# Fused attention and two feed-forward blocks on one core: sums of the exponentials with a DVE addition, and other queues

## The chip, the cores and the metric

One core of one Trainium2 chip. The metric is the device time of the kernel in microseconds (us), median over runs. Engines: PE (TensorE matmul; PEld is its weight load), DVE (VectorE), ACT (ScalarE), POOL (GpSimd) and SP (SyncE, which here only issues DMAs).

## The reference

Attention with a tanh cap over 2 x 12 heads (sequence 448, head size 64), then two feed-forward blocks without biases (768 to 2048 to 768), the first with h·cos(h), the second with silu. All in float32, to float32 accuracy.

```python
scores = scale * np.matmul(q, k.transpose(0, 1, 3, 2))
scores = cap * np.tanh(scores / cap)
scores = scores - np.max(scores, axis=-1, keepdims=True)
attn = np.exp(scores)
attn = attn / (np.sum(attn, axis=-1, keepdims=True) + 1e-09)
o = np.matmul(attn, v)                 # then heads side by side: x, (896, 768)
h = x @ w_in;   x2 = (h * np.cos(h)) @ w_out
h = x2 @ w2_in; y  = (h / (1.0 + np.exp(-h))) @ w2_out
```

## The kernel before, in words

The 24 heads go in 12 pairs p; the two heads u of a pair share the 128 partitions. The order of every engine's work is written out by hand (a manual schedule), so each engine's queue is the order of the code.

**Scores.** Keys of a head are cut into three blocks of 128 and a rest of 64. `S_pe(p, t)` computes scores transposed (keys on partitions, the 448 queries on the free axis). For t = 0 to 2 these are block t of both heads, one PSUM bank per head, from q and k split in two float32r parts (`qk_split`, L215 and L216 on DVE): three products per head, each on 64 rows of the array, the two heads on the two row halves (L232). For t = 3 it is the rest of both heads in one bank, straight from `raw` in float32, on two column halves (L236). `ps_s` has three buffers of two banks; a fourth score tile waits for the tanh of the first. `S_tanh` (L244) and `S_exp` (L250) on ACT leave the exponentials in `e32[p]`, seven chunks of 448: chunk 2t+u is block t of head u, chunk 6 the rest, head 0 on partitions 0 to 63 and head 1 on 64 to 127. No maximum is subtracted, since the cap bounds the scores.

**P·V and sums.** `PV(p, steps)` (L262) adds V-transposed times the exponentials into the bank `po`: per step t two float32 matmuls, head u on column half u. Step 3 uses chunk 6 for both heads, with V chunks 6 and 7, whose other half is zeros. `PV_sums` (L275) makes the sums over the keys with matmuls of ones into the bank `sm`: two steps of four matmuls, each on a quarter of 32 columns; quarter c belongs to head c // 2, and the two quarters of a head are added later on DVE. `ps_o` has one bank for `po` and one for `sm`. A float32 matmul leaves two records in the trace, so a step of P·V has four and a step of sums eight.

**Evacuation and normalising.** `evac` copies `po` (L281), `evac_sums` copies `sm` (L286) and sends one row of each quarter with a DMA of its own from SP's queue (L290), four a pair, to `sums[p]` as 32 partitions of 28. `recip(p)` (L296, L297) adds the two halves, takes the reciprocal, writes it to DRAM (`rs`, L299) and reads it back spread over the partitions (`rb`, two DMAs, L302), all on SP. `norm_mul` and `norm_split` (L308, L315, L316) multiply and split the result into the two float32r parts of `x`, the input of the first matrix product.

**Order of a turn.** A loop over p (L359) is software-pipelined: turn p issues the load of pair p+3 (POOL's queue from pair 3 on), the load of V for p+1 (SP), scores, tanh and exponentials of p+1, `recip(p-2)`, `qk_split(p+2)`, the steps of early weights, normalising of p-3, then P·V, `evac`, sums and `evac_sums` of p. In turn 11 the sums and their evacuation come ahead of P·V, and `recip(10)` ahead of the normalising of pair 8. `early` spreads the preparation of the first three weights (a guard and a hi part on ACT; floor, three bit steps and a lo part on DVE) over turns 2 to 10, and a load of the next weight from POOL.

**Ahead of the loop** pair 0 is made: exponentials in two pieces (chunks 0 to 3, then 4 to 6), a `warm_up` of four matmuls with zeros, P·V steps 0 and 1 and one step of sums.

**Behind the loop** `gemm_in` starts: 36 matmuls (L419) with `x` of batch 0 (pairs 0 to 5), 24 with pairs 6 to 9, then 12 with pairs 10 and 11, and so on; from there on the weights stream in and PE works without a break.

Of the kernel before, what the change touches and what calls it, by code (L numbers as in the profile page):

```python
# [28 lines left out]
F32 = mybir.dt.float32  # L29
# [4 lines left out]
ALU = mybir.AluOpType  # L34
# [3 lines left out]
def tile_attention_ffn_ffn(  # L38
# [10 lines left out]
    nc = tc.nc  # L49
    B, H, S, D = shape  # L50
    DM = out.shape[1]
    DFF = w_in1.shape[0] * 128
    P = 128
# [10 lines left out]
    const = ctx.enter_context(tc.tile_pool(name="const", bufs=1))  # L64
# [94 lines left out]
    with ExitStack() as actx:  # L159
        dpool = actx.enter_context(tc.tile_pool(name="dr", bufs=2, space=bass.MemoryType.DRAM))  # L160
        ap_ = actx.enter_context(tc.tile_pool(name="att", bufs=2))
        ps_s = actx.enter_context(tc.tile_pool(name="ps_s", bufs=3, space=PSUM))
        ps_o = actx.enter_context(tc.tile_pool(name="ps_o", bufs=1, space=PSUM))
        NPT = NHEAD // 2
        NCH = 7
        NV = NCH + 1
        Q = 32
        KB = S + 64
        QK = S + KB
        W = 64  # L170
        FULL = S + S // P * P
        FIRST = S + P
        PAD = 16

        raw, vf = {}, {}


        ones = const.tile([P, 3, Q], F32, name="ones")

        def v_init():  # L180
            nc.gpsimd.memset(ones[:, 0], 1.0)
            for u in range(2):
                for h in range(2):
                    nc.gpsimd.memset(ones[h * D:(h + 1) * D, 1 + u], float(u == h))

# [12 lines left out]
        def load_v(p):  # L200
            if p >= NPT:
                return
            vf[p] = ap_.tile([P, NV, D], F32, tag="vf", name=f"vf{p}", bufs=2)
            nc.sync.dma_start(vf[p].rearrange("p c d -> p (c d)"), qkv[p][:, PAD + QK:])

        qh, ql = {}, {}

        def qk_split(p, part=slice(0, FULL)):
            if p >= NPT:
                return  # L210
            if p not in qh:
                qh[p] = ap_.tile([P, FULL], F32R, tag="qh", name=f"qh{p}", bufs=2)
                ql[p] = ap_.tile([P, FULL], F32R, tag="ql", name=f"ql{p}", bufs=2)
            h, x = qh[p][:, part], raw[p][:, PAD:][:, part]
            nc.vector.tensor_copy(h, x)  # L215
            nc.vector.tensor_tensor(out=ql[p][:, part], in0=x, in1=h.bitcast(F32), op=ALU.subtract)  # L216

        sc, e32 = {}, {}

        def S_pe(p, t):  # L220
            if p >= NPT:
                return
            ps = ps_s.tile([P, 2, 512], F32, tag="sc", name=f"sc{p}_{t}")
            sc[p, t] = ps
            h, l = qh.get(p), ql.get(p)
            ops = ((h, h), (h, l), (l, h))
            if t < 3:
                cols = slice(S + t * P, S + (t + 1) * P)
                for m, (kk, qq) in enumerate(ops):
                    for u in range(2):  # L230
                        rows = slice(u * D, (u + 1) * D)
                        nc.tensor.matmul(ps[:, u, :S], kk[rows, cols], qq[rows, :S], start=m == 0, stop=m == 2)  # L232
            else:
                x = raw[p][:, PAD:]
                for c in range(0, P, W):
                    nc.tensor.matmul(ps[c:c + W, 0, :S], x[:, FULL + c:FULL + c + W], x[:, :S], start=True, stop=True)  # L236

        def S_tanh(p, t):
            if p >= NPT:
                return  # L240
            if t == 0:
                e32[p] = ap_.tile([P, NCH, S], F32, tag="e32", name=f"e32_{p}", bufs=2)
            n = 2 if t < 3 else 1
            nc.scalar.activation(out=e32[p][:, 2 * t:2 * t + n, :], in_=sc.pop((p, t))[:, :n, :S], func=AF.Tanh, scale=scap)  # L244

        def S_exp(p, chunks=slice(0, NCH)):
            if p >= NPT:
                return
            e = e32[p][:, chunks, :]
            nc.scalar.activation(out=e, in_=e, func=AF.Exp, scale=capt)  # L250

        po_, sm_ = {}, {}


        def PV(p, steps):
            first = p not in po_
            if first:
                po_[p] = ps_o.tile([P, 512], F32, tag="po", name=f"po{p}")[:, :S]
            for n, t in enumerate(steps):
                for c in range(0, P, W):  # L260
                    u, f = divmod(c, D)
                    nc.tensor.matmul(po_[p][c:c + W], vf[p][:, 2 * t + u, f:f + W], e32[p][:, min(2 * t + u, NCH - 1), :],  # L262
                                     start=first and n == 0, stop=t == 3)


        def PV_sums(p, steps):
            first = p not in sm_
            if first:
                sm_[p] = ps_o.tile([P, 512], F32, tag="sm", name=f"sm{p}")[:, :S]
            for n, t in enumerate(steps):  # L270
                for c in range(4):
                    u, x = divmod(c, 2)
                    chunk = 4 * t + 2 * x + u
                    one = ones[:, 0] if chunk < NCH - 1 else ones[:, 1 + u]
                    nc.tensor.matmul(sm_[p][c * Q:(c + 1) * Q], one, e32[p][:, min(chunk, NCH - 1), :], start=first and n == 0, stop=t == 1)  # L275

        xu, sums, rb = {}, {}, {}

        def evac(p):
            xu[p] = ap2.tile([P, S], F32, tag="xu", name=f"xu{p}", bufs=4)  # L280
            nc.vector.tensor_copy(xu[p], po_.pop(p))  # L281

        def evac_sums(p):
            x = ap2.tile([P, S], F32, tag="xs", name=f"xs{p}", bufs=2)
            sums[p] = ap2.tile([32, 2, S // 16], F32, tag="sums", name=f"sums{p}", bufs=2)
            nc.vector.tensor_copy(x[:3 * Q + 1], sm_.pop(p)[:3 * Q + 1])  # L286
            for u in range(2):
                for y in range(2):
                    at = u * D + y * Q
                    nc.sync.dma_start(sums[p][16 * u:16 * u + 16, y], x[at:at + 1])  # L290

        def recip(p):
            if p < 0:
                return
            s = sums.pop(p)
            nc.vector.tensor_tensor(out=s[:, 0], in0=s[:, 0], in1=s[:, 1], op=ALU.add)  # L296
            nc.vector.reciprocal(out=s[:, 0], in_=s[:, 0])  # L297
            d = dpool.tile([2, S], F32, tag="rs", name=f"rs{p}")
            nc.sync.dma_start(d.rearrange("h (a n) -> (h a) n", a=16), s[:, 0])  # L299
            r = ap2.tile([P, S], F32, tag="rb", name=f"rb{p}", bufs=4)  # L300
            for u in range(2):
                nc.sync.dma_start(r[u * D:(u + 1) * D, :], d[u:u + 1].to_broadcast([D, S]))  # L302
            rb[p] = r

        def norm_mul(p):
            if p < 0:
                return
            nc.vector.tensor_tensor(out=rb[p], in0=xu.pop(p), in1=rb[p], op=ALU.mult)  # L308
# [12 lines left out]
        def warm_up(n, ps):  # L321
            for _ in range(n):
                nc.tensor.matmul(ps, zero[:, :P], zero, start=True, stop=True)


        early = {}
        for w, turn in ((0, 2), (1, 4), (2, 6)):
            for at, *step in ((0, w_guard, w, None), (1, w_floor, w, nc.vector), (1, w_bits, w, 0), (2, w_bits, w, 1), (2, w_bits, w, 2),
                              (2, w_load, w + 2, nc.gpsimd), (3, w_hi, w), (4, w_lo, w)):
                early.setdefault(turn + at, []).append(step)  # L330
        early.setdefault(NPT - 2, []).append((w_guard, 3, None))
        early.setdefault(NPT - 1, []).append((w_floor, 3, nc.gpsimd))
# [16 lines left out]
        for t in range(4):  # L349
            S_pe(0, t)  # L350
            S_tanh(0, t)
            if t == 1:
                S_exp(0, slice(0, 4))
        S_exp(0, slice(4, NCH))
        qk_split(1)
        warm_up(4, ps_o.tile([P, 512], F32, tag="sm", name="warm1")[:, :S])
        PV(0, [0, 1])
        PV_sums(0, [0])
        for p in range(NPT):  # L359
            load(p + 3)  # L360
            if p > 0:
                load_v(p + 1)
            for t in range(3):
                S_pe(p + 1, t)
                S_tanh(p + 1, t)
            S_pe(p + 1, 3)
            S_tanh(p + 1, 3)
            S_exp(p + 1)
            recip(p - 2)
            qk_split(p + 2)  # L370
            for f, *a in early.get(p, []):
                f(*a)
            if p == NPT - 1:
                recip(p - 1)
            norm_mul(p - 3)
            norm_split(p - 3)
            if p == NPT - 1:
                PV_sums(p, [0, 1])
                evac_sums(p)
            PV(p, range(4) if p else [2, 3])  # L380
            evac(p)
            if p < NPT - 1:
                PV_sums(p, [0, 1] if p else [1])
                evac_sums(p)
        norm_mul(NPT - 3)
        norm_split(NPT - 3)
        recip(NPT - 1)
# [263 lines left out]
```

## Time and profile before

| what | us |
|---|---|
| median of 3 runs | 581.74 |
| runs, lowest to highest | 581.37 to 588.43 |
| profiled execution, time | 580.33 |
| profiled execution, span first to last instruction | 578.5 |
| PE busy in the span | 567.1 |
| DVE / ACT / POOL busy | 379.9 / 265.1 / 155.7 |

All rows come from the one profiled execution; its own time (580.33) is its span and what lies around it. In rows, "x16" is a count of records, a mean or the length of a merged group stands in front, and brackets say how long the engine was idle before and what it waited for. Ends of matmuls are modelled; starts are records.

### The profile page before, as it was taken

To read this page: it belongs to the slowest core of one execution; us is meant where nothing else is said; L and a number is where in the kernel's file an instruction comes from. 1 tells how busy PE (TensorE), PEld (TensorE's weight loads), DVE (VectorE), ACT (ScalarE), POOL (GpSimd) and SP (SyncE) were. 2 spreads that over 40 slices of the span, in tenths; PEclk is the share of its full clock that TensorE was granted. 3 is DMA by queue.
4 is the path that set the end of the run, shared out by engine and by line. 5 is a ranking of instruction groups with operands and counts; after the bars stand their busy time and mean duration, and the time that the engine had idled before them with its cause. 6 is when DMAs were issued, how large, how long until landed. Compare 5 with 4: busy or idle time off the path is not lost.

```text
span 578.5 us, 7770 instructions
## 1 busy us (share of the span) xinstructions
PE 567.1 (98%) x3060; PEld 486.7 (84%) x3060; DVE 379.9 (66%) x490; ACT 265.1 (46%) x307; POOL 155.7 (27%) x84
## 2 busy tenths in 40 slices
PE   8999999889999999999999999999999999999997
PEld 4444443779999999999999999999999999999997
DVE  3356885489998888667646552888877866644501
ACT  6989985167777766233323222433333323232201
POOL 1001101033444433242332221344222223313300
PEclk9999999989999999999999999999999999999999
DMA  7245642123333323343433330343333334443102
GB/s 282 88 123 175 185 133 71 48 78 104 132 126 109 110 92 101 101 145 93 134 110 108 109 127 30 114 148 121 109 110 109 110 110 137 136 141 121 53 1 95
DMA packets 18755, 65.51 MB, mean 113 GB/s; under 512 B 4192, under 2 KB 7776, under 8 KB 18720
## 3 DMA queue, kind: packets, MB, share of 16 engines
q1 hardware_dynamic: 17280, 57.95, 31.1%
q0 software_dynamic: 1152, 6.78, 3.4%
q8 instruction: 24, 0.39, 0.3%
q10 hardware_dynamic: 288, 0.30, 0.2%
q14 instruction: 11, 0.09, 0.0%
HBM read 62.14 MB, written 2.80 MB: 112 GB/s over the span
## 4 chain that ended last, share of the span: by engine, by line
PE 88%; DMA 6%; DVE 2%; ACT 2%; SPq 1%; issue 0%; DVEq 0%
PE h L419 38%; PE o L566 20%; PE y L419 20%; PE po L262 4%; PE sc L232 2%; DMA rs<-sums 2%; DMA rb<-rs 2%; PE sm L275 2%; PE sc L236 1%; ACT e L244 1%; ACT e L250 1%; DMA raw<-in_qkv 1%; SPq L290 1%; SPq L302 1%; DMA sums<-xs 0%
## 5 line engine op out<-in xcount | busy, mean ns | idle before, releaser
L120 POOL TENSOR_SCALAR w<-w 128x768 f32<-128x768 f32 (+1 forms) x63 | 148.2, 2352 | 315.5 <-ACT w L114 251.4
L419 PE MATMUL h<-x,whi 128*128 128x448 f32 x768 | 219.6, 367 | 3.9 <-DVE x L315 3.7
L419 PEld LDWEIGHTS h<-x,whi 128*128 128x128 f32 x768 | 145.0, 189 | 16.9 <-DVE x L315 4.0
L419 PE MATMUL h<-x,wlo 128*128 128x448 f32 x384 | 140.9, 367 | 0.0
L144 ACT ACTIVATE whi<-w 128x768 fp32r<-128x768 f32 (+1 forms) x66 | 54.3, 823 | 144.0 <-DVE w L136 133.4
L566 PE MATMUL o<-whi,g 128*128 128x384 f32 x448 | 114.3, 335 | 0.0
L419 PE MATMUL y<-g,whi 128*128 128x448 f32 x384 | 109.2, 366 | 0.0
L133 DVE SCALAR_TENSOR_TENSOR w<-w,wraw 128x768 int32<-128x768 int32 (+1 forms) x66 | 61.6, 933 | 43.5 <-POOL w L120 42.5
L151 DVE TENSOR_TENSOR wlo<-w,whi 128x768 fp32r<-128x768 f32 (+1 forms) x66 | 61.4, 931 | 31.7 <-ACT whi L144 30.9
L566 PEld LDWEIGHTS o<-whi,g 128*128 128x128 f32 x448 | 81.0, 188 | 0.0
L419 PEld LDWEIGHTS h<-x,wlo 128*128 128x128 f32 x384 | 72.6, 189 | 5.7
L419 PEld LDWEIGHTS y<-g,whi 128*128 128x128 f32 x384 | 72.1, 188 | 5.9
L566 PE MATMUL o<-wlo,g 128*128 128x384 f32 x224 | 75.1, 335 | 0.0
L419 PE MATMUL y<-g,wlo 128*128 128x448 f32 x192 | 70.2, 366 | 0.0
L136 DVE SCALAR_TENSOR_TENSOR w<-wraw,w 128x768 uint32<-128x768 uint32 (+1 forms) x66 | 61.6, 934 | 2.3
L131 DVE TENSOR_SCALAR wraw<-wraw 128x768 int32<-128x768 int32 (+1 forms) x66 | 56.0, 849 | 9.7 <-ACT w L114 9.7
L114 ACT ACTIVATE w<-wraw 128x768 f32<-128x768 f32 (+1 forms) x66 | 58.0, 879 | 3.4 <-DMA wraw<-in_moe_w_out 3.4
L244 ACT ACTIVATE e<-sc,scap 128x896 f32<-128x896 f32 (+1 forms) x48 | 40.0, 913 | 12.1 <-PE sc L232 12.1
L566 PEld LDWEIGHTS o<-wlo,g 128*128 128x128 f32 x224 | 42.0, 188 | 0.0
L475 ACT ACTIVATE r<-h 128x896 f32<-128x896 f32 (+1 forms) x18 | 14.8, 835 | 58.7 <-PE h L419 56.8
L262 PE MATMUL po<-e,vf 128*64 128x448 f32 x192 | 38.5, 541 | 0.7 <-ACT e L250 0.5
L419 PEld LDWEIGHTS y<-g,wlo 128*128 128x128 f32 x192 | 36.1, 188 | 3.0
(54 smaller groups left out, 398.4 us busy)
## 6 DMA issues: line engine op xcount, KB each, us to landing
wraw<-in_moe_w_in SPq DMA_DIRECT2D x29, 768.0 KB, 4.3
wraw<-in_moe_w_out SPq DMA_DIRECT2D x22, 768.0 KB, 4.3
wraw<-in_moe_w_out SPq DMA_DIRECT2D x12, 640.0 KB, 4.0
raw<-in_qkv POOLq DMA_DIRECT2D x9, 480.0 KB, 4.5
vf<-in_qkv SPq DMA_DIRECT2D x12, 256.0 KB, 3.3
rb<-rs SPq DMA_DIRECT2D x24, 112.0 KB, 2.9
out<-os SPq DMA_DIRECT2D x13, 192.0 KB, 1.9
wraw<-in_moe_w_in POOLq DMA_DIRECT2D x3, 768.0 KB, 5.2
```

What stands on the lines that cost most here:

```text
L114: nc.scalar.activation(out=w32[i][:, :n, :].bitcast(F32), in_=wraw[i][:, :n, :, 1].bitcast(F32), func=AF.Abs, scale=2.0 ** -48)
L120: eng.tensor_scalar(out=t, in0=t, scalar1=2.0 ** -63, scalar2=None, op0=ALU.max)
L131: nc.vector.tensor_scalar(out=w1, in0=w1, scalar1=-0x80000000, scalar2=None, op0=ALU.bitwise_and)
L133: nc.vector.scalar_tensor_tensor(out=t, in0=t, scalar=3, in1=w1, op0=ALU.logical_shift_left, op1=ALU.bitwise_or)
L136: nc.vector.scalar_tensor_tensor(out=t, in0=w0.bitcast(U32), scalar=29, in1=t, op0=ALU.logical_shift_right, op1=ALU.bitwise_or)
L144: nc.scalar.activation(out=whi[i][:, :n, :], in_=w32[i][:, :n, :].bitcast(F32), func=AF.Copy)
L151: nc.vector.tensor_tensor(out=wlo[i][:, :n, :], in0=w32.pop(i)[:, :n, :].bitcast(F32), in1=whi[i][:, :n, :].bitcast(F32), op=ALU.subtract)
L244: nc.scalar.activation(out=e32[p][:, 2 * t:2 * t + n, :], in_=sc.pop((p, t))[:, :n, :S], func=AF.Tanh, scale=scap)
L262: nc.tensor.matmul(po_[p][c:c + W], vf[p][:, 2 * t + u, f:f + W], e32[p][:, min(2 * t + u, NCH - 1), :], start=first and n == 0, stop=t == 3)
L419: nc.tensor.matmul(pt, l, r, start=first and m == 0, stop=last and m == len(ops) - 1)
L475: nc.scalar.activation(out=r, in_=h, func=AF.Silu)
L566: nc.tensor.matmul(pt[t], l, r[:, cols], start=k == 0 and m == 0, stop=k == KF - 1 and m == 2)
```

## The change

- **Sums.** On DVE a new addition `e_add(p)` makes `e01` = chunks 0 and 1 plus chunks 2 and 3. `PV_sums` is then one step of four quarters (`e01` and chunks 4 and 5 of each head). The rest chunk 6 goes in a new `PV_mixed`: for each row half two matmuls of 64 rows by 64 columns, one with V into `po`, one with ones (32 columns of ones, 32 of zeros) into the other head's half of `sm`. The zero-padded V chunk is gone: V has 7 chunks. In `sm` the heads are now swapped, which `recip` undoes when it reads `rs`.
- **Order.** Step 3 of P·V becomes `PV_mixed`; turns 0 to 10 issue P·V steps, mixed step, `evac`, sums, `evac_sums`; turn 11 issues mixed step, sums, `evac_sums`, P·V, `evac`, and `recip(10)` comes behind them. `sm` of pair 11 takes a buffer of `ps_s`.
- **Queues.** The sums of a pair go out as two DMAs, on POOL's queue (pair 11: ACT's). V of pairs 2 and up is loaded from POOL's queue. Of pair 11 the DMAs of `recip` are on ACT's queue.
- **First turn.** Exponentials of pair 0 in three pieces; no second warm-up; the first score step of pair 1 ahead of P·V step 1 of pair 0.
- **Early weights** start a turn earlier for weight 0, and the later steps of each come a turn later.

```diff
         ps_o = actx.enter_context(tc.tile_pool(name="ps_o", bufs=1, space=PSUM))
         NPT = NHEAD // 2
         NCH = 7
-        NV = NCH + 1
         Q = 32
         KB = S + 64
         QK = S + KB
...
         raw, vf = {}, {}
-        ones = const.tile([P, 3, Q], F32, name="ones")
+        ones = const.tile([P, 3 * Q], F32, name="ones")
         def v_init():
-            nc.gpsimd.memset(ones[:, 0], 1.0)
-            for u in range(2):
-                for h in range(2):
-                    nc.gpsimd.memset(ones[h * D:(h + 1) * D, 1 + u], float(u == h))
+            nc.gpsimd.memset(ones[:, :2 * Q], 1.0)
+            nc.gpsimd.memset(ones[:, 2 * Q:], 0.0)
...
         def load_v(p):
             if p >= NPT:
                 return
-            vf[p] = ap_.tile([P, NV, D], F32, tag="vf", name=f"vf{p}", bufs=2)
-            nc.sync.dma_start(vf[p].rearrange("p c d -> p (c d)"), qkv[p][:, PAD + QK:])
+            vf[p] = ap_.tile([P, NCH, D], F32, tag="vf", name=f"vf{p}", bufs=2)
+            (nc.gpsimd if p > 1 else nc.sync).dma_start(vf[p].rearrange("p c d -> p (c d)"), qkv[p][:, PAD + QK:])
         qh, ql = {}, {}
...
         po_, sm_ = {}, {}
-        def PV(p, steps):
-            first = p not in po_
-            if first:
-                po_[p] = ps_o.tile([P, 512], F32, tag="po", name=f"po{p}")[:, :S]
+        def acc(d, p, tag):
+            if p in d:
+                return d[p], False
+            t = ps_o.tile([P, 512], F32, tag=tag, name=f"{tag}{p}") if p < NPT - 1 or tag == "po" else ps_s.tile([P, 2, 512], F32, tag="sc", name=f"{tag}{p}")[:, 0]
+            d[p] = t[:, :S]
+            return d[p], True
+        def PV(p, steps, last=False):
+            po, first = acc(po_, p, "po")
             for n, t in enumerate(steps):
-                for c in range(0, P, W):
-                    u, f = divmod(c, D)
-                    nc.tensor.matmul(po_[p][c:c + W], vf[p][:, 2 * t + u, f:f + W], e32[p][:, min(2 * t + u, NCH - 1), :],
-                                     start=first and n == 0, stop=t == 3)
-        def PV_sums(p, steps):
-            first = p not in sm_
-            if first:
-                sm_[p] = ps_o.tile([P, 512], F32, tag="sm", name=f"sm{p}")[:, :S]
-            for n, t in enumerate(steps):
-                for c in range(4):
-                    u, x = divmod(c, 2)
-                    chunk = 4 * t + 2 * x + u
-                    one = ones[:, 0] if chunk < NCH - 1 else ones[:, 1 + u]
-                    nc.tensor.matmul(sm_[p][c * Q:(c + 1) * Q], one, e32[p][:, min(chunk, NCH - 1), :], start=first and n == 0, stop=t == 1)
+                for u in range(2):
+                    nc.tensor.matmul(po[u * D:(u + 1) * D], vf[p][:, 2 * t + u, :], e32[p][:, 2 * t + u, :],
+                                     start=first and n == 0, stop=last and n == len(steps) - 1)
+        def PV_mixed(p, last=False):
+            po, first = acc(po_, p, "po")
+            sm, _ = acc(sm_, p, "sm")
+            for u in range(2):
+                rows, other = slice(u * D, (u + 1) * D), slice((1 - u) * D, (2 - u) * D)
+                e = e32[p][rows, NCH - 1, :]
+                nc.tensor.matmul(po[rows], vf[p][rows, NCH - 1, :], e, start=first, stop=last)
+                nc.tensor.matmul(sm[other], ones[rows, Q:], e, start=True, stop=False)
+        def PV_sums(p):
+            sm, _ = acc(sm_, p, "sm")
+            x = e01.pop(p)
+            for c, e in enumerate((x[:, 1], e32[p][:, 5, :], x[:, 0], e32[p][:, 4, :])):
+                nc.tensor.matmul(sm[c * Q:(c + 1) * Q], ones[:, :Q], e, start=False, stop=True)
+        e01 = {}
+        def e_add(p):
+            if p >= NPT:
+                return
+            e01[p] = ap_.tile([P, 2, S], F32, tag="e01", name=f"e01_{p}", bufs=2)
+            nc.vector.tensor_tensor(out=e01[p], in0=e32[p][:, 0:2, :], in1=e32[p][:, 2:4, :], op=ALU.add)
         xu, sums, rb = {}, {}, {}
...
             x = ap2.tile([P, S], F32, tag="xs", name=f"xs{p}", bufs=2)
             sums[p] = ap2.tile([32, 2, S // 16], F32, tag="sums", name=f"sums{p}", bufs=2)
             nc.vector.tensor_copy(x[:3 * Q + 1], sm_.pop(p)[:3 * Q + 1])
-            for u in range(2):
-                for y in range(2):
-                    at = u * D + y * Q
-                    nc.sync.dma_start(sums[p][16 * u:16 * u + 16, y], x[at:at + 1])
+            for y in range(2):
+                (nc.gpsimd if p < NPT - 1 else nc.scalar).dma_start(sums[p][:, y], x[y * Q:y * Q + D + 1:D])
         def recip(p):
             if p < 0:
...
             nc.vector.tensor_tensor(out=s[:, 0], in0=s[:, 0], in1=s[:, 1], op=ALU.add)
             nc.vector.reciprocal(out=s[:, 0], in_=s[:, 0])
             d = dpool.tile([2, S], F32, tag="rs", name=f"rs{p}")
-            nc.sync.dma_start(d.rearrange("h (a n) -> (h a) n", a=16), s[:, 0])
+            eng = nc.sync if p < NPT - 1 else nc.scalar
+            eng.dma_start(d.rearrange("h (a n) -> (h a) n", a=16), s[:, 0])
             r = ap2.tile([P, S], F32, tag="rb", name=f"rb{p}", bufs=4)
             for u in range(2):
-                nc.sync.dma_start(r[u * D:(u + 1) * D, :], d[u:u + 1].to_broadcast([D, S]))
+                eng.dma_start(r[u * D:(u + 1) * D, :], d[1 - u:2 - u].to_broadcast([D, S]))
             rb[p] = r
         def norm_mul(p):
...
         early = {}
-        for w, turn in ((0, 2), (1, 4), (2, 6)):
-            for at, *step in ((0, w_guard, w, None), (1, w_floor, w, nc.vector), (1, w_bits, w, 0), (2, w_bits, w, 1), (2, w_bits, w, 2),
-                              (2, w_load, w + 2, nc.gpsimd), (3, w_hi, w), (4, w_lo, w)):
+        for w, turn in ((0, 1), (1, 4), (2, 6)):
+            for at, *step in ((0, w_guard, w, None), (1, w_floor, w, nc.vector), (1, w_bits, w, 0), (2, w_bits, w, 1), (3, w_bits, w, 2),
+                              (3, w_load, w + 2, nc.gpsimd), (4, w_hi, w), (5, w_lo, w)):
                 early.setdefault(turn + at, []).append(step)
         early.setdefault(NPT - 2, []).append((w_guard, 3, None))
         early.setdefault(NPT - 1, []).append((w_floor, 3, nc.gpsimd))
...
         for t in range(4):
             S_pe(0, t)
             S_tanh(0, t)
-            if t == 1:
-                S_exp(0, slice(0, 4))
+            if t < 2:
+                S_exp(0, slice(2 * t, 2 * t + 2))
         S_exp(0, slice(4, NCH))
         qk_split(1)
-        warm_up(4, ps_o.tile([P, 512], F32, tag="sm", name="warm1")[:, :S])
-        PV(0, [0, 1])
-        PV_sums(0, [0])
+        e_add(0)
+        PV(0, [0])
+        S_pe(1, 0)
+        S_tanh(1, 0)
+        PV(0, [1])
         for p in range(NPT):
             load(p + 3)
             if p > 0:
                 load_v(p + 1)
-            for t in range(3):
+            for t in range(0 if p else 1, 3):
                 S_pe(p + 1, t)
                 S_tanh(p + 1, t)
             S_pe(p + 1, 3)
             S_tanh(p + 1, 3)
             S_exp(p + 1)
             recip(p - 2)
+            if p > 0:
+                e_add(p)
             qk_split(p + 2)
             for f, *a in early.get(p, []):
                 f(*a)
-            if p == NPT - 1:
-                recip(p - 1)
             norm_mul(p - 3)
             norm_split(p - 3)
-            if p == NPT - 1:
-                PV_sums(p, [0, 1])
+            if p < NPT - 1:
+                PV(p, [0, 1, 2] if p else [2])
+                PV_mixed(p, True)
+                evac(p)
+                PV_sums(p)
                 evac_sums(p)
-            PV(p, range(4) if p else [2, 3])
-            evac(p)
-            if p < NPT - 1:
-                PV_sums(p, [0, 1] if p else [1])
+            else:
+                PV_mixed(p)
+                PV_sums(p)
                 evac_sums(p)
+                PV(p, [0, 1, 2], True)
+                evac(p)
+        recip(NPT - 2)
         norm_mul(NPT - 3)
         norm_split(NPT - 3)
         recip(NPT - 1)
...
-    qkv = np.zeros((n, P, pad + S + full + 128 + 8 * D), np.float32)
+    qkv = np.zeros((n, P, pad + S + full + 128 + 7 * D), np.float32)
...
-        at = pad + S + full + 128 + (6 + u) * D
-        qkv[:, u * 64:(u + 1) * 64, at:at + D] = v[:, u, full:]
+        qkv[:, u * 64:(u + 1) * 64, -D:] = v[:, u, full:]
```

## Rows read from the trace of the kernel before

**Rows 1.** The page: busy time of each engine, its share, instructions.

```profile
PE 567.1 (98%) x3060; PEld 486.7 (84%) x3060; DVE 379.9 (66%) x490; ACT 265.1 (46%) x307; POOL 155.7 (27%) x84
```

**Rows 2.** Busy time by stretch; after POOL: PE's granted clock, DMA share, GB/s.

```profile
0.00:101.06 101.06, 97.21 (x660) 44.05 (x661) 60.17 (x112) 82.01 (x70) 9.67 (x22) 1.00 0.47 151
...
26.42:34.01 7.59, 7.59 (x58) 3.40 (x54) 3.12 (x6) 6.64 (x6) 0.54 (x1) 1.00 0.34 101
26.42:95.42 69.00, 68.84 (x490) 31.00 (x486) 49.47 (x91) 61.28 (x52) 5.01 (x9) 1.00 0.46 139
34.01:87.78 53.77, 53.61 (x383) 24.21 (x380) 41.19 (x75) 47.63 (x41) 4.48 (x8) 1.00 0.50 152
95.42:101.06 5.64, 4.80 (x33) 1.56 (x33) 1.68 (x4) 0.35 (x1) 2.12 (x1) 1.00 0.18 55
101.06:121.60 20.54, 16.69 (x75) 14.69 (x73) 11.46 (x23) 4.44 (x7) 0.15 (x1) 0.92 0.12 35
165.00:180.00 15.00, 15.00 (x76) 13.90 (x74) 13.69 (x16) 11.14 (x13) 6.79 (x3) 1.00 0.37 131
```

**Rows 3.** PE in order of time, end of turn 0 to turn 2: start, length.

```profile
17.17 0.96 PE L275 MATMUL sm<-e,ones 128*32 128x448 f32 x8
18.06 0.47 PE L232 MATMUL sc<-qh 64*128 64x448 f32 x2
...
20.87 0.97 PE L236 MATMUL sc<-raw 128*64 128x448 f32 x4 [0.70 <-ACT e L244]
21.68 3.18 PE L262 MATMUL po<-e,vf 128*64 128x448 f32 x16
24.78 1.71 PE L275 MATMUL sm<-e,ones 128*32 128x448 f32 x16
26.42 0.47 PE L232 MATMUL sc<-qh 64*128 64x448 f32 x2
26.73 0.36 PE L232 MATMUL sc<-ql,qh 64*128 64x448 f32 x2
26.93 0.36 PE L232 MATMUL sc<-qh,ql 64*128 64x448 f32 x2
```

**Rows 4.** ACT in order of time, exponentials of pair 0.

```profile
8.35 1.79 ACT L250 ACTIVATE e<-e,capt 128x1792 f32<-128x1792 f32 x1
...
11.59 1.42 ACT L250 ACTIVATE e<-e,capt 128x1344 f32<-128x1344 f32 x1
13.65 3.33 ACT L244 ACTIVATE e<-sc,scap 128x896 f32<-128x896 f32 x4 [0.65 <-PE sc L232]
```

**Rows 5.** Line L438: lengths in ns (lowest, median, highest), first and last start, forms.

```profile
L438 DVE TENSOR_TENSOR g<-r,g x36: 614/1084/1747, 127.8 to 460.3; 128x896 fp32r<-128x896 f32 x28, 128x448 fp32r<-128x448 f32 x8
```

**Rows 6.** DVE, then SP's queue, then PE in order of time, at the hand-over.

```profile
103.02 0.62 DVE L286 COPY xs<-sm 97x448 f32<-97x448 f32 x1
...
111.30 0.17 DVE L296 TENSOR_TENSOR sums<-sums 32x28 f32<-32x28 f32 x1 [4.22 <-DMA sums<-xs]
...
116.67 0.63 DVE L308 TENSOR_TENSOR rb<-xu,rb 128x448 f32<-128x448 f32 x1 [3.29 <-DMA rb<-rs]
...
117.76 0.63 DVE L316 TENSOR_TENSOR x<-rb,x 128x448 fp32r<-128x448 f32 x1
...
106.59 2.49 SPq L290 DMA_DIRECT2D sums<-xs  x4
111.85 0.31 SPq L299 DMA_DIRECT2D rs<-sums  x1
113.17 1.12 SPq L302 DMA_DIRECT2D rb<-rs  x2
...
117.78 0.47 PE L419 MATMUL h<-x,whi 128*128 128x448 f32 x1 [3.67 <-DVE x L315]
```

**Rows 7.** DMA: loads from POOL (size, median us to landing); landing of the sums.

```profile
raw<-in_qkv POOLq DMA_DIRECT2D x9, 480.0 KB, 4.5
...
DMA to landing us min/median/max: 1.3/2.2/5.2
```

## The prediction

> **What bounds the kernel now.** I read the page's busy line first: TensorE is busy 567.1 of 578.5 us [rows 1], so only work taken off PE, or PE's 11.4 us of idle time, can pay. The second view, busy time by stretch [rows 2], says where: 3.9 us idle before 101.06 (the attention turns and the start), 3.9 us between 101.06 and 121.60 (the hand-over to the first matrix product); 3.7 us remain for the 457 us behind it. In the nine turns from 26.42 to 95.42 (turns p = 2 to 10) PE is busy 68.84 of 69.00, ACT 61.28, DVE 49.47: the attention is PE-bound at 7.67 us a turn, with ACT 0.9 us a turn behind. The third view is PE in order of time [rows 3]. A turn is nine score pairs (26.42 to about 28.4), the raw scores (L236, 0.81 from 20.87 to 21.68), four steps of P·V (3.10 from 21.68 to 24.78), two steps of sums (1.64 to 26.42). One step of sums alone takes 0.89 (17.17 to 18.06). So a step costs 0.75 and a change from one tile shape to the next some 0.14.
>
> The hand-over is read from DVE, SP and PE there [rows 6]. The sums of pair 11 leave DVE at 103.02, but their four DMAs stand on SP behind the broadcast of pair 9 and go out at 106.59; DVE waits 4.22 for them, 3.29 for the broadcast, and PE 3.67 at 117.78. Behind the wait the granted clock is down: the stretch averages 0.92 of the full level of 2.4 GHz [rows 2]. The 72 matmuls of L419 there would take 72 x 0.2035 = 14.65 us at the pace of 165 to 180 (74 weight loads in 15.00 us) [rows 2]; they take 20.54. The tail costs 5.9 us.
>
> **The change, part by part.**
>
> *PE work of a turn.* Sums fall from two steps to one: 1.64 - 0.89 = -0.75. P·V keeps three steps, 3.10 - 0.75 = 2.35. The fourth becomes the mixed step: two 64x64 matmuls of V and two of ones, on the four quarters of the array. No row shows that form. Lower bound: all four side by side, one step, 0.75 plus a shape change, 0.87. Upper bound: one after another, 4 x 0.75 = 3.0. Nearest rows: the score matmuls use both row halves at once (0.36 us each, a pair every 0.20) and the sums all four column quarters at once (eight records in 0.89) [rows 3]. I take 0.87. New turn: 2.0 + 0.81 + 2.35 + 0.87 + 0.89 = 6.92, with the small launch gaps 6.97, against 7.59 in a plain turn [rows 2]: 0.62 less.
> The rows show row halves together only where they write different PSUM banks (L232 writes a bank per head). The Trainium skill, "TensorEngine Tiling (Array Packing)", section "Restrictions and Gotchas", says that different row tiles cannot access the same PSUM bank at the same time; here both row halves write `po`, and both write `sm`, on different partitions. By that rule the mixed step would run in two pairs; no row before tests it, and it is the first rival below.
>
> *ACT.* Its 61.28 us in nine turns are 6.8 a turn [rows 2], just below 6.97. The weight steps are spread over one turn more, so single turns may be held by ACT by 0.2 to 0.3 us; I add 0.3 in all.
>
> *The addition on DVE (e_add).* 128 x 896 f32 from two inputs: the same size at L438 takes 1.08 median, 0.61 (half size) to 1.75 [rows 5]; I take 1.08, range 1.0 to 1.75. DVE is busy 41.19 us in turns 3 to 9 [rows 2]; plus 7 x 1.08 that is 48.8, and seven new turns of PE are 7 x 6.97 = 48.8. DVE is full in those turns. It costs nothing as long as `evac` of a turn may be late: `po` is wanted again only after the scores of the next turn, 2.8 us later [rows 3], and DVE enters turn 3 early, since turns 0 to 2 have no normalising yet. At 1.75 DVE would need 4.7 us more than PE, about 2 beyond that cover.
>
> *Queues.* `sums` goes from four SP issues a pair to two on POOL, and V loads (p > 1) follow. Behind a `sums` DMA on POOL, which waits for `evac_sums`, now stand the next raw load and V load. The raw load goes out about 2 us into the turn instead of in the middle of the turn before; it lands in 4.5 us [rows 7] and is split in the next turn, near 2.5 us into it, about 3 us of cover. `sums` lands in 1.3 to 5.2 us, median 2.2 [rows 7], and has a whole turn. SP keeps only the reciprocal's way out and in, so the waits for `rb` which cost PE some 0.7 us in the nine turns (69.00 against 9 x 7.59) go. Cost taken: 0.
>
> *Start.* Exponentials in three pieces: from the two lengths (1.79 for 1792, 1.42 for 1344 elements) a piece of 896 is about 1.05, so two cost 0.3 more than one of 1792 [rows 4]. Scores of pair 1 start ahead of the second P·V step, so ACT's 0.65 us wait at 13.65 goes. ACT is 0.4 to 0.5 earlier; so is PE in turn 1, where L236 waits for ACT at 20.87 [rows 3]. The dropped warm-up stood in a wait for ACT and gives nothing. Turn 2 starts at 20.4 + 0.81 + 2.35 + 0.87 + 0.89 = 25.3 instead of 26.42.
>
> *Turns 2 to 10*: 25.3 + 9 x 6.97 + 0.3 = 88.3 instead of 95.42.
>
> *Turn 11.* Before: 5.64, of them 0.84 idle [rows 2] for the `sm` bank. Now `sm` has a bank of its own, but the sums wait for exp, then for e_add: mixed step 0.87, a wait of about 1.1, sums 0.89, P·V 2.35, sum 5.2. L419 starts at 93.5 instead of 101.06: 7.5 earlier.
>
> *Hand-over.* On DVE behind exp (88.3): e_add 1.1, a weight step 1, normalising of pair 8 1.7 (116.67 to 118.39 [rows 6]), `evac_sums` 0.6: 92.7. ACT's queue is free, two issues and a landing as at the last two of SP (0.6 + 2.7): 96.0. `recip` 0.5; out and back 1.3 and 3.5 (111.85 to 113.17 to 116.67 [rows 6]): 101.3; normalising of pairs 10 and 11: x is ready near 103.5. `recip(10)`, now behind `evac(11)`, starts near 93.9 and is back by 100. PE wants x of pairs 10 and 11 after 60 and 63 matmuls: 93.5 + 12.2 = 105.7 and 106.3. The wait is covered with about 2.5 us to spare, and with no gap the clock stays: the 72 matmuls end at 93.5 + 14.65 = 108.1 instead of 121.60, 13.5 earlier.
>
> *Behind it* PE is full and the weights' preparation starts earlier with it; the gain stays. Rounded down: 13.4. The profiled execution took 580.33 (span 578.5 and 1.8 around it); 580.33 - 13.4 = 566.9. The median shown, 581.74, is 1.4 above the profiled one; I forecast a median of 568.3.
>
> **Rivals.**
> 1. *Mixed step in two pairs* (row halves that share a bank exclude each other): 0.75 more in each of 11 turns, 8.3: 576.6. For: no row shows both halves in one bank. Against: the writes go to different partitions. The page cited above would have this one.
> 2. *DVE becomes the bound*: e_add at 1.5 to 1.75, or POOL's DMA work beside it lengthens DVE; 2 to 4 us lost: about 571. For: 48.8 of 48.8. Against: the late `evac` is covered.
> 3. *The hand-over still ends on a DMA*: sums landing at 5.2 instead of 2.7 and the way out at 2.6 use up the 2.5 us, then a gap of 1.5 and a lowered clock behind it (2 us here): 571 to 572.
> 4. *Slower: the mixed step runs its four matmuls one after another*, 2.25 over the forecast in 12 turns, 27 us: 568.3 + 27 = 595. It decides from a mixed step of 0.87 + 13.4 / 12 = 2.0 us on. For: quarters by rows and columns at once are not in the trace. Against: each axis alone runs side by side [rows 3].
> 5. *The change does less than it says* (no PE time saved, hand-over alone): 575; taken with the first.
>
> **Chances.** Forecast 0.56 (its own range 565.0 to 570.1), rival 2 0.13, rival 3 0.13, rivals 1 and 5 0.13, rival 4 0.05. A measurement of this kernel tells about 2% from no change: below 570.1 is faster. Some of rivals 2 and 3 fall below it: faster 0.61, same 0.34, slower 0.05. The range takes in rivals 1 to 3: 564.0 to 576.6.
>
> **What would show it.** In the changed profile: nine score pairs of successive turns 6.9 to 7.1 us apart; the mixed step near 0.87 (0.9 to 1.0 supports it, 1.6 is rival 1, 3 is rival 4); e_add near 1.1 and no wait of P·V for `xu`; L419 beginning at 93 to 94.5 with no idle time for x of pairs 10 and 11 and a granted clock of 1.00 there. A gap at L419 is rival 3; turns of 7.3 and more with PE waiting for DVE in turns 6 to 9 are rival 2. The forecast is wrong if turns save less than 0.4, or the hand-over keeps over 2 us of idle time.

## The result, and the profile after

The changed kernel takes 567.2 us in the median of four runs (567.13 to 567.84), against a forecast of 568.3; ratio to the kernel before 0.9727, 95% interval 0.9656 to 0.9797. Its profiled execution took 567.21 us (span 565.2) where 566.9 was forecast, against 580.33 (578.5) before.

The page's busy line, against [rows 1]:

```profile
PE 556.3 (98%) x3008; PEld 479.9 (85%) x3008; DVE 393.4 (70%) x502; ACT 264.9 (47%) x308; POOL 179.8 (32%) x113
```

PE is 10.8 us less busy, DVE 13.5 more. Busy time by stretch, against [rows 2] (columns as there): the start and the attention; turns 2 to 10; turns 3 to 9; turn 11; the first 72 matmuls of the first product (now L439); the rest.

```profile
0.00:93.69 93.69, 88.55 (x608) 38.40 (x609) 73.76 (x128) 81.76 (x71) 34.88 (x51) 1.00 0.51 160
...
25.13:87.97 62.84, 62.84 (x454) 27.30 (x450) 57.07 (x99) 59.69 (x51) 26.90 (x37) 1.00 0.55 161
...
32.13:80.99 48.86, 48.86 (x354) 21.24 (x350) 46.90 (x81) 46.48 (x40) 21.85 (x30) 1.00 0.55 166
87.97:93.69 5.72, 4.42 (x32) 1.14 (x29) 5.48 (x10) 1.76 (x3) 4.37 (x3) 1.00 0.11 28
93.69:108.38 14.69, 14.69 (x72) 13.63 (x73) 9.78 (x20) 4.85 (x8) 0.59 (x1) 1.00 0.12 39
...
108.40:565.20 456.80, 453.08 (x2329) 427.89 (x2327) 309.80 (x356) 178.31 (x230) 144.29 (x62) 1.00 0.34 108
```

and the rest of the kernel before:

```profile
121.60:578.50 456.90, 453.21 (x2329) 427.96 (x2327) 308.32 (x357) 178.66 (x231) 145.92 (x62) 1.00 0.33 108
```

Nine turns take 62.84 us instead of 69.00; L439 begins at 93.69 instead of 101.06; its first 72 matmuls take 14.69 at a full granted clock where they took 20.54 at 0.92. From there to the end it is 456.8 us, 456.9 before. So the 13.3 us of span are 1.3 up to the start of turn 2 (25.13 against 26.42), 6.2 in nine turns, 5.85 in the hand-over, and a little given back in turn 11 (5.72 against 5.64).

PE in order of time, end of turn 0 and P·V of turn 1, against [rows 3] (start, length):

```profile
15.66 0.59 PE L273 MATMUL po<-e,vf 64*64 64x448 f32 x1
15.67 0.59 PE L274 MATMUL sm<-e,ones 64*64 64x448 f32 x1
15.68 0.59 PE L273 MATMUL po<-e,vf 64*64 64x448 f32 x1
15.68 0.59 PE L274 MATMUL sm<-e,ones 64*64 64x448 f32 x1
...
16.58 0.96 PE L281 MATMUL sm<-e,ones 128*32 128x448 f32 x8
...
20.97 2.42 PE L263 MATMUL po<-e,vf 128*64 128x448 f32 x12
```

The four matmuls of the mixed step start within 0.02 us, and the sums begin 0.92 us behind the first. P·V is three steps, the sums one. Where DVE is latest, in turn 7, its copy of `po` (`evac`) starts 1.3 us after that step; PE does not wait for it:

```profile
67.47 0.62 DVE L295 COPY xu<-po 128x448 f32<-128x448 f32 x1
```

In turn 11 PE waits 0.19 us for the exponentials, then for `e_add`, then for the first bank of L439:

```profile
90.16 0.96 PE L281 MATMUL sm<-e,ones 128*32 128x448 f32 x8 [0.95 <-DVE e L289]
91.05 2.48 PE L263 MATMUL po<-e,vf 128*64 128x448 f32 x12
...
93.69 0.67 PE L439 MATMUL h<-x,whi 128*128 128x448 f32 x2 [0.16 <-DVE xs L300]
```

DVE and ACT's queue at the hand-over, against [rows 6]:

```profile
93.02 0.62 DVE L300 COPY xs<-sm 97x448 f32<-97x448 f32 x1
...
96.66 0.17 DVE L308 TENSOR_TENSOR sums<-sums 32x28 f32<-32x28 f32 x1
...
103.04 0.63 DVE L321 TENSOR_TENSOR rb<-xu,rb 128x448 f32<-128x448 f32 x1 [1.92 <-DMA rb<-rs]
...
93.67 1.74 ACTq L302 DMA_DIRECT2D sums<-xs  x2
97.22 0.34 ACTq L312 DMA_DIRECT2D rs<-sums  x1
```

The sums of pair 11 leave 10 us earlier (93.02 against 103.02) and their DMAs go out 0.65 us after the copy starts, not 3.57. x of pair 11 is normalised from 103.04 and ready at 104.7; PE comes to it after 63 matmuls, near 106.5, and does not wait.

Some executions of most of these kernels end 6 to 7 us later than the others, and in the three traces of such (run 1 and the second runs of 5 and 8) the matmuls of the first products take 368 instead of 365 ns at a full granted clock; below, times are those of the others unless it says so.

### The profile page after: what moved, and what is told of

It reads as the page before. It is cut to its first block, busy times and chain, and to the rows that moved or that the text cites. A ratio compares the mean times of both kernels' runs of the same rounds, so it can differ in the third digit from the quotient of the medians.

```text
span 565.2 us, 7664 instructions
## 1 busy us (share of the span) xinstructions
PE 556.3 (98%) x3008; PEld 479.9 (85%) x3008; DVE 393.4 (70%) x502; ACT 264.9 (47%) x308; POOL 179.8 (32%) x113
## 4 chain that ended last, share of the span: by engine, by line
PE 95%; ACT 2%; DVE 1%; issue 1%; DMA 1%
PE h L439 41%; PE o L586 21%; PE y L439 21%; PE po L263 4%; PE sc L229 3%; PE sc L233 2%; PE sm L281 2%; PE po L273 2%; ACT e L241 1%; ACT e L247 1%; DMA raw<-in_qkv 1%; DVE e L289 0%; DVE x L328 0%; DVE wlo L151 0%; DVE ql L213 0%
## 5 line engine op out<-in xcount | busy, mean ns | idle before, releaser
L439 PE MATMUL h<-x,whi 128*128 128x448 f32 x768 | 218.1, 365 | 0.2 <-DVE xs L300 0.2
L439 PEld LDWEIGHTS h<-x,whi 128*128 128x128 f32 x768 | 144.2, 188 | 12.4 <-DVE xs L300 0.9
L439 PE MATMUL h<-x,wlo 128*128 128x448 f32 x384 | 140.2, 365 | 0.0
L439 PE MATMUL y<-g,whi 128*128 128x448 f32 x384 | 109.2, 366 | 0.0
L439 PEld LDWEIGHTS y<-g,whi 128*128 128x128 f32 x384 | 72.1, 188 | 5.8
L439 PEld LDWEIGHTS h<-x,wlo 128*128 128x128 f32 x384 | 72.1, 188 | 5.7
L439 PE MATMUL y<-g,wlo 128*128 128x448 f32 x192 | 70.2, 366 | 0.0
L131 DVE TENSOR_SCALAR wraw<-wraw 128x768 int32<-128x768 int32 (+1 forms) x66 | 57.9, 877 | 9.0 <-ACT w L114 9.0
L439 PEld LDWEIGHTS y<-g,wlo 128*128 128x128 f32 x192 | 36.1, 188 | 3.0
L458 DVE TENSOR_TENSOR g<-r,g 128x896 fp32r<-128x896 f32 (+1 forms) x36 | 37.5, 1049 | 0.3 <-ACT g L489 0.3
```

What stands on the lines that cost most here:

```text
L131: nc.vector.tensor_scalar(out=w1, in0=w1, scalar1=-0x80000000, scalar2=None, op0=ALU.bitwise_and)
L439: nc.tensor.matmul(pt, l, r, start=first and m == 0, stop=last and m == len(ops) - 1)
L458: nc.vector.tensor_tensor(out=gl, in0=r, in1=gh.bitcast(F32), op=ALU.subtract)
```

## The experiments

**1. The mixed step on two quarters instead of four.**

```diff
-nc.tensor.matmul(sm[other], ones[rows, Q:], e, start=True, stop=False)
+nc.tensor.matmul(sm[rows], ones[rows, Q:], e, start=True, stop=False)
```

(and the two heads' quarters of the sums and of `rs` changed back to match)

> The mixed step with the ones of each head on the same quarter of the array as its V (the head's own half of sm) instead of the free quarter. Theory (the step is short because its four matmuls stand on four different quarters): two by two on one quarter, the step takes 1.6 instead of 0.92 us, a turn 7.7 instead of 6.98, in all 12 x 0.75 = 9 us more: 576.2. Rival (the step's length has to do with its few rows or with launches, not with the quarters): no change, 567.2. Rival (the banks exclude each other as well): above 580.

Measured: 575.3 us (five executions, 575.0 to 575.6), 8.1 more. PE in order of time, one turn:

```profile
31.57 0.98 PE L273 MATMUL po<-e,vf 64*64 64x448 f32 x4
32.38 0.93 PE L274 MATMUL sm<-e,ones 64*64 64x448 f32 x4
33.23 0.96 PE L281 MATMUL sm<-e,ones 128*32 128x448 f32 x8
```

Now V goes first and the ones 0.81 behind it: the step takes 1.66 instead of 0.92 us, a turn 7.73 (20.70 to 90.23 in nine) instead of 6.98. So the four free quarters are what makes the step short. It is less than 9 because not all twelve steps show: nine turns give 6.7, the stretch from there to L439 0.74 for two steps (of turn 11's, a part stands in PE's wait for `e_add`, 0.47 here instead of 0.95), and turn 0's stands in a wait for ACT. Of the rest, 0.47 is the start (first tanh at 6.61 in this profile, 6.14 in the changed kernel's).

**2. The old arithmetic under the new order and queues** (four steps of P·V with the padded V, two steps of sums, no `e_add`).

```diff
-PV(p, [0, 1, 2] if p else [2]); PV_mixed(p, True); evac(p); PV_sums(p)
+PV(p, [0, 1, 2, 3] if p else [2, 3]); evac(p); PV_sums(p, [0, 1])
```

> The changed kernel with the old arithmetic: four full steps of P.V, two steps of sums, no e_add; new queues, order of turn 11, start and early weights stay. Theory (the PE work of a turn and the hand-over are two separate gains): turns back to 7.59, 11 x 0.62 = 6.8 us more, hand-over still covered with no idle time for x: 573.5 to 574. Rival (the hand-over is only covered because the shorter turns come with it): a gap at L419 comes back, 578 and more. Rival (the gain came from the queues alone): 567 to 568.

Measured: 572.2 us (five executions, 572.0 to 572.8), 5.0 more. The first product begins with no wait, and PE does not wait for x behind it either:

```profile
98.65 0.67 PE L421 MATMUL h<-x,whi 128*128 128x448 f32 x2
```

Its turns are 7.57 against 6.98 (20.24 to 88.38 in nine, against 20.17 to 83.01). The expectation counted 11 turns at 0.62; nine count at 0.59, 5.3, and turn 11 gives 0.4 back, since the old sums wait for no addition. The hand-over is covered without the arithmetic, by order and queues: 580.33 - 572.2 = 8.1 of the 13.1 us come from these, the start and the early weights.

**3. The new arithmetic alone in the kernel before** (mixed step, `e_add`, one step of sums; everything else as before).

> The kernel before with the new arithmetic alone: mixed step, e_add, one step of sums; queues (four DMAs of the sums and V on SP), order of turn 11, start and early weights as before. Theory (SP's queue was next to its limit: 2.4 sums + 0.5 V + 0.4 out + about 2.6 wait + 1.1 back = 7.1 us a turn): turns end at 7.1 to 7.3 with waits for rb on DVE, and the hand-over keeps its gap of 4 us or more: 576 to 579. Rival (the parts simply add, SP is no limit): turns 6.97, 581.65 - 6.8 = 574.8. Rival (nothing of the PE time arrives): 581.

Measured: 577.3 us in its profile (seven executions, 576.2 to 579.0), ratio to the kernel before 0.9946, interval 0.9896 to 0.9996. PE in order of time (idle before, and what ended it):

```profile
57.99 2.48 PE L262 MATMUL po<-e,vf 128*64 128x448 f32 x12 [2.09 <-DMA vf<-in_qkv]
65.58 2.48 PE L262 MATMUL po<-e,vf 128*64 128x448 f32 x12 [0.39 <-DVE xu L294]
74.40 2.48 PE L262 MATMUL po<-e,vf 128*64 128x448 f32 x12 [1.62 <-DVE xu L294]
82.81 2.48 PE L262 MATMUL po<-e,vf 128*64 128x448 f32 x12 [1.21 <-DVE xu L294]
...
115.94 0.47 PE L438 MATMUL h<-x,whi 128*128 128x448 f32 x1 [2.34 <-DVE x L328]
```

From turn 1 to turn 5 P·V begins every 6.98 us; in turn 6 it begins 9.24 after the last. There PE waits for a V load that stood late on SP (again in turn 11, 1.39 us), in turns 7 to 9 for DVE, which waits for `rb`, as here in turn 8:

```profile
72.09 0.63 DVE L321 TENSOR_TENSOR rb<-xu,rb 128x448 f32<-128x448 f32 x1 [2.15 <-DMA rb<-rs]
```

SP's queue where turn 5 goes over into turn 6:

```profile
50.08 1.13 SPq L315 DMA_DIRECT2D rb<-rs  x2
51.31 2.74 SPq L303 DMA_DIRECT2D sums<-xs  x4
54.15 1.54 SPq L201 DMA_DIRECT2D vf<-in_qkv  x1
55.73 0.43 SPq L312 DMA_DIRECT2D rs<-sums  x1
58.04 1.13 SPq L315 DMA_DIRECT2D rb<-rs  x2
```

From one `rb` to the next it is 7.96 us, of which 2.3 lie between the way out (`rs`) and the way back. Alone the arithmetic is worth about 3.1 us (580.33 against 577.25), in the new order 5.0: shorter turns need the relieved queue. Little of the 3.1 is won in the turns: L438 begins at 100.57, only 0.5 earlier than before. The rest lies in the hand-over, where PE waits 2.34 us instead of 3.67 and the granted clock stays at 1.00 behind it.

**4. `e_add` done twice.**

```diff
 nc.vector.tensor_tensor(out=e01[p], in0=e32[p][:, 0:2, :], in1=e32[p][:, 2:4, :], op=ALU.add)
+nc.vector.tensor_tensor(out=e01[p], in0=e32[p][:, 0:2, :], in1=e32[p][:, 2:4, :], op=ALU.add)
```

> The addition e_add is done twice, 0.95 us more on DVE in each turn, nothing else. Theory (DVE is full in turns 3 to 9, with a cover of about 1 to 2 us left): PE begins to wait for po and sm in turns 6 to 9; seven turns at 0.95 less the cover, 5 to 6 us more: 572 to 573. Rival (DVE has room, its addition is hidden whatever it takes): under 1 us more. Rival (no cover at all): 7 to 11 us more.

Measured: 577.5 us (eight executions, 577.1 to 578.7), 10 more; the expectation of 5 to 6 was too low. The number lies in the range of the rival without any cover, but not for that rival's reason. The first product starts at 104.00, 10.3 later. The turns lose what was expected: `evac` of turn 10 comes at 93.52 instead of 87.20, 6.3 later, with PE waiting for `xu` four times, 2.8 us in all, and for ACT once, 0.8. The other 4 us come in turn 11, where the addition is not hidden at all. PE in order of time:

```profile
98.11 1.72 PE L281 MATMUL sm<-e,ones 128*32 128x448 f32 x8 [2.88 <-DVE e L290]
99.76 4.32 PE L263 MATMUL po<-e,vf 128*64 128x448 f32 x12
```

and busy time of that stretch (columns as in [rows 2]):

```profile
98.11:104.00 5.89, 5.89 (x20) 1.44 (x20) 2.90 (x5) 0.00 (x0) 0.30 (x1) 0.54 0.12 40
```

PE waits 2.88 us for it (0.95 in the changed kernel; 0.9 of the difference is that the second addition takes 1.97 here), and behind that wait the granted clock is 0.54, near the level of 1.2 GHz: the sums take 1.72 instead of 0.96, P·V 4.32 instead of 2.48, together 2.60 more. This wait is paid nearly twice.

**5. Two DMAs of the sums, V and all of pair 11 on SP.**

```diff
-(nc.gpsimd if p < NPT - 1 else nc.scalar).dma_start(sums[p][:, y], x[y * Q:y * Q + D + 1:D])
+nc.sync.dma_start(sums[p][:, y], x[y * Q:y * Q + D + 1:D])
```

> The changed kernel with the queues of before: V, the sums' two DMAs and all of pair 11 on SP. Theory (two DMAs instead of four leave SP 1.2 sums + 0.5 V + 0.3 out + 1.4 to 3 wait + 1.1 back = 4.5 to 6.1 us a turn, under 6.98; in the hand-over the order on SP is the order of need): turns unchanged, within 0.6 us: 567.2 to 567.8. Rival (the choice of POOL and ACT as queues is what covers the hand-over): a gap of 2 us or more, with the clock behind it 570 and up.

> V, the sums' two DMAs and all of pair 11 on SP, once more: its single profile stood 0.4 us above the changed kernel, its other executions 6 to 9 above. Theory (two DMAs are what matters, not the queue): undisturbed executions within 1 us of the changed kernel of this call. Rival (SP's queue costs time in most executions, by waits for rb that the one profile did not have): 3 us and more above it in all executions but a few.

Measured: 567.73 the first time and 567.85 the second, one execution each; the changed kernel beside the second has 567.47. The other six of its eight executions took 574.4 to 577.3. The trace kept of one of them (574.58) shows nearly the same attention: turns are 6.98, PE waits for DVE once more, in turn 11, and L439 starts at 94.68 against 94.01.

```profile
89.30 0.56 PE L273 MATMUL po<-e,vf 64*64 64x448 f32 x1 [0.85 <-DVE xu L295]
```

The other 6.4 us of that execution lie behind L439, where PE waits for no DMA of the attention. By the traces, moving the DMAs to POOL and ACT is worth 0.4 to 0.7 us. Why so many executions are long here, and none of the ten of the changed kernel, is open. Two of them (577.02 and 577.29) also have a mean granted clock of 0.995 and 0.996, below the 0.999 and 1.000 of the changed kernel, and left no trace. So the second expectation's rival, that SP's queue costs time in most executions, is not ruled out.

**6. The same with four DMAs on SP**, as before.

> As the run before, but the sums of a pair go out as four DMAs on SP, as in the kernel before; arithmetic, order of turn 11, start as changed. Theory (SP needs some 7.1 us a turn where PE needs 6.98): DVE waits for rb in most turns, the sums of pair 10 go out late, and the hand-over has a gap of 1 to 4 us: 569 to 573. Rival (four DMAs are as good as two): 567 to 568.

Measured: 575.0 us in its profile (573.9 to 575.7 in three), 7 more: above the expectation, and not by a gap in front of x, which isn't there. DVE waits for `rb` (2.33, 0.49, 1.19, 2.23, 1.59 us from turn 5 on), turns from 5 on take 7.3 to 7.8, and turn 11 has two waits of PE with a lowered clock behind them. P·V of turn 10 starts 2.9 us later than in the changed kernel; the other 4.7 up to the first product are lost from there on, 3.0 of them by that clock (sums and P·V). DVE, then PE in order of time:

```profile
90.82 0.62 DVE L323 TENSOR_TENSOR rb<-xu,rb 128x448 f32<-128x448 f32 x1 [2.23 <-DMA rb<-rs]
...
93.17 0.56 PE L273 MATMUL po<-e,vf 64*64 64x448 f32 x1 [2.16 <-DVE xu L295]
...
95.03 1.72 PE L281 MATMUL sm<-e,ones 128*32 128x448 f32 x8 [0.88 <-DVE e L289]
96.68 4.73 PE L263 MATMUL po<-e,vf 128*64 128x448 f32 x12
```

and busy time of the last stretch:

```profile
96.00:101.30 5.30, 5.30 (x17) 1.24 (x12) 2.18 (x4) 0.00 (x0) 0.00 (x0) 0.50 0.16 38
```

Runs 5 and 6 differ only in two against four DMAs a pair, and that is worth about 7 us: the number of issues counts here, far more than the engine that issues them, as far as run 5 tells.

**7. `recip` of pair 10 ahead, as before**, in turn 11.

```diff
+if p == NPT - 1:
+    recip(p - 1)
 norm_mul(p - 3)
```

> The changed kernel, but in turn 11 recip of pair 10 stands ahead of the normalising of pair 8 on DVE, as in the kernel before. Theory (DVE waits in order for the sums of pair 10, which go out at about 89.0 to 90.2 and land near 92; evac_sums of pair 11, which L419's first bank waits for, comes 1.5 to 2 us later): L419 starts 1 to 2 us later, x of pair 11 stays covered: 568 to 569.5. Rival (the order on DVE was the cause of the gap before): a gap for x comes back, 571 and more. Rival: no change.

Measured: 568.1 us (four executions, 567.95 to 569.75), 0.9 above the changed kernel, 0.6 above its second measurement (run 8). DVE waits 0.87 for the sums of pair 10, `evac_sums` comes at 94.00 instead of 93.02, and L439's first bank holds PE:

```profile
94.67 0.67 PE L440 MATMUL h<-x,whi 128*128 128x448 f32 x2 [0.99 <-DVE xs L300]
```

This order on DVE alone does not bring back the gap for x; it is worth the 0.8 us by which PE waits longer here (0.99 against 0.16). That the larger part of the old wait was SP's lateness is read from [rows 6], where the DMAs of pair 11's sums go out 3.57 us after their copy starts, and is not shown by a run of its own: run 6, with four DMAs on SP, has no such gap, but there PE itself comes to x late, behind the lowered clock.

**8. A version that beats both**: in turn 11 two steps of P·V ahead of the sums, and `evac_sums` ahead of the normalising of pair 8.

```diff
 PV_mixed(p)
+PV(p, [0, 1])
 PV_sums(p)
 evac_sums(p)
-PV(p, [0, 1, 2], True)
+norm_mul(p - 3)
+norm_split(p - 3)
+PV(p, [2], True)
```

> A version meant to beat both: in turn 11 two steps of P.V stand between the mixed step and the sums, so that PE does not wait for e_add (0.95 us in the trace), and evac_sums stands ahead of the normalising of pair 8 on DVE, so that L419's first bank is free in time (0.16 us). Theory: 1.0 to 1.1 us less, x of pairs 10 and 11 still covered: 566.1 to 566.3. Rival (the chain of pair 11 or of x is in the way of it): no gain or a small loss, 567.2 to 568.

> The changed kernel once more, unchanged, beside the three runs below on the same chip, since single executions begin up to 0.5 us apart. Expected: 567.1 to 567.9.

> The version with two steps of P.V ahead of the sums in turn 11 and evac_sums ahead of the normalising of pair 8, once more beside the changed kernel. Theory: 1.0 to 1.1 us below the changed kernel of this call. Rival (0.16 and 0.95 us of idle time were not on the path): within 0.3 us of it.

Measured: 567.2 us the first time (five executions, 566.5 to 567.5), no less than the changed kernel in the result above; the second time, beside the changed kernel with 567.47 (567.3 to 568.4), 566.2 (five executions, 565.95 to 566.6): 1.2 less, as expected. PE in order of time in the first profile: sums behind two steps, no wait, and the first product behind the last step.

```profile
89.57 1.72 PE L263 MATMUL po<-e,vf 128*64 128x448 f32 x8
91.22 0.96 PE L281 MATMUL sm<-e,ones 128*32 128x448 f32 x8
92.11 0.97 PE L263 MATMUL po<-e,vf 128*64 128x448 f32 x4
93.01 0.67 PE L443 MATMUL h<-x,whi 128*128 128x448 f32 x2
```

**9. The start of before in the changed kernel** (exponentials in two pieces, second warm-up, scores of pair 1 behind both P·V steps).

> The changed kernel with the start of before: exponentials of pair 0 in two pieces, the second warm-up, the first score step of pair 1 behind both P.V steps of pair 0. Theory (ACT's wait of 0.65 us at the start is what the new start saves, and ACT sets the end of turn 1): 0.4 to 0.7 us more, all of it by turn 2. Rival (turn 1 hides it): no change. Rival (pieces cost more than they save): 0.3 us less.

Measured: 566.9 us (four executions, 566.7 to 567.2), 0.6 less than the changed kernel beside it (567.47). The expectation had the sign wrong; its last rival (pieces cost more than they save) had it right. ACT in order of time, this kernel:

```profile
6.11 1.91 ACT L241 ACTIVATE e<-sc,scap 128x896 f32<-128x896 f32 x2 [3.44 <-PE sc L229]
8.05 1.79 ACT L247 ACTIVATE e<-e,capt 128x1792 f32<-128x1792 f32 x1
...
12.61 3.31 ACT L241 ACTIVATE e<-sc,scap 128x896 f32<-128x896 f32 x4
```

and the changed kernel beside it:

```profile
6.48 1.01 ACT L241 ACTIVATE e<-sc,scap 128x896 f32<-128x896 f32 x1 [3.81 <-PE sc L229]
7.53 1.04 ACT L247 ACTIVATE e<-e,capt 128x896 f32<-128x896 f32 x1
...
13.32 3.31 ACT L241 ACTIVATE e<-sc,scap 128x896 f32<-128x896 f32 x4
```

From the first tanh of pair 0 to that of pair 1 it is 6.50 us with two pieces, 6.84 with three. ACT does not wait with the old start either: what it waited for in [rows 4], the step of sums between P·V and the scores of pair 1, is gone with the arithmetic. The extra piece costs its 0.34 us and saves nothing. The other 0.3 or so is the first load, which landed 0.37 us earlier in this execution. This start together with version 8 was not tried.

## Why the prediction was right

- *PE work of a turn.* Forecast 6.97, measured 6.98; mixed step forecast 0.87, measured 0.92. The 0.3 us added for ACT did not come: in turns 2 to 10 PE is busy for all of the 62.84. The first rival (pairs) and the fourth (one after another) fall: run 1 shows what the step costs when quarters are shared: 1.66 us, and 8.1 in all where rival 1 had 8.3.
- *The bank rule.* The four starts within 0.02 us, in a step no longer than 0.92, show both row halves writing `po` at the same time, on different partitions, and both writing `sm`. The Trainium skill, "TensorEngine Tiling (Array Packing)", section "Restrictions and Gotchas", excludes that for one PSUM bank; here the measurement differs, and it decides.
- *DVE.* `e_add` takes 1.02 (forecast 1.08), DVE is busy 46.90 of 48.86 us in turns 3 to 9 (48.8 of 48.8), and `evac` starts at most 1.3 us after the mixed step's end (67.47 in turn 7), inside the cover of 2.8. Rival 2 did not come; run 4 shows how near it was.
- *Queues.* Cost 0 held, though the two DMAs of most pairs take 1.7 us to issue on POOL, where two of SP's four took 1.25 ([rows 6]). That SP would be relieved was right, and larger than I had it: I put 0.7 us on its waits; runs 3 and 6 show that the shorter turns would have lost 2 to 7 us on the old queue.
- *Start.* Turn 2 begins at 25.13 (25.3). The sum was right and its reason wrong: I gave the removal of ACT's 0.65 us wait to the new start; run 9 shows that the missing step of sums removes it, and that the smaller pieces cost 0.34. And 0.27 of the 1.29 us won by then is luck: the first load landed earlier in this execution (first tanh at 6.14, 6.41 before).
- *Turn 11.* From the mixed step to L439 5.46 (88.23 to 93.69) against 5.2. The wait for `e_add` is 0.95 (1.1); the term missed is L439's first bank, which `sm` of pair 11 holds until `evac_sums`: 0.16.
- *Hand-over.* L439 at 93.69 (93.5), x of pair 11 from 103.04 (ready near 103.5, measured 104.7), 72 matmuls done at 108.4 (108.1). Rival 3 did not come: about 1.8 us were left.
- *The median.* 567.2 against 568.3: I carried over the 1.4 us by which the median before stood above its profile, but the changed kernel's four executions lie within 0.7. The kernel before spreads wider: of its executions beside the experiments, three with a mean granted clock of 1.000 took 575.9 to 578.0, all with 0.993 to 0.997 at least 579.2. They left no trace; that the clock in the hand-over makes this difference is likely and not shown.

## What to carry to other kernels

A matmul with few rows and few columns can share its step with three others if each stands on a quarter of the array of its own; sharing a quarter costs the whole step again. When PE work is taken out of a loop, count the issues and waits of each DMA queue per turn first: the shorter turn here fits only because a queue that was nearly full was relieved with it (run 6); two DMAs a pair fewer were enough for that (run 5). At a hand-over between stages follow the last result's chain queue by queue, and look for work that can stand between it and the engine that waits.

## What the runs showed of the hardware that was not expected

- Waits on PE of 0.95 and 0.16 us (the changed kernel), of 1.39 and 0.84 in one turn and one of 2.34 (run 3) left the granted clock at 1.00; waits of 0.96 and 2.88 in one turn (run 4) were followed by 0.54 over 5.9 us, and of 2.16 and 0.88 (run 6) by 0.50 over 5.3.
- A DVE addition of 1.02 to 1.09 us took 1.97 in the one place where POOL worked on a tile beside it (run 4, turn 11), and a DVE cast of mostly 0.39 took 0.90 beside POOL in the changed kernel (91.54); a two-input product there kept its 0.61 (90.90). That POOL is the cause was not tested.
- Two DMAs of 3.5 KB took 1.73 us to issue on POOL in eight pairs and 1.2 in three, 1.74 on ACT (the changed kernel), and 1.17 on SP (run 5).
